# Twelve more first products in blocks, masks on GpSimd, and a refitted issue order in an attention and mixture kernel

## Chip, cores and metric

One core of a Trainium2 chip runs one program. The metric is device microseconds from launch to end, the median of several runs. Lower is better.

## The reference

Four batches of 768 tokens go through an attention of 8 heads (64 wide), and the result through four dense experts that are mixed by per-token shares.

```python
scores = (q @ k.T) / sqrt(D)
keep = (key < 4) | ((0 <= query - key) & (query - key < 128))      # 4 sinks and a window of 128
a = softmax(where(keep, scores, -1e9))
x = (a @ v)                                  # 3072 tokens x 512 (heads side by side)
p = domain_probs / (domain_probs.sum(-1) + 1e-9)
for e in range(4):
    h = maximum(x @ w1[e], 0)                # 512 -> 1024
    out += p[:, e] * (h @ w2[e])             # 1024 -> 512
```

## The kernel before, in words

Everything is in bf16 with f32 accumulation. A batch has 3 groups of 256 tokens, so there are 12 pairs (batch b, group g), and with 4 experts e 48 units (b, g, e). The first product of a unit is x @ w1[e], the second h @ w2[e].

**Attention.** Scores are made per group and pair of heads (`scores`, line 634 to 640), with keys on the partitions. ScalarE takes the exponential into the tile aT (L665). The window is then cut out by a mask: in batch 0 partly by a bias in PSUM or a multiplication of each head (L674), in batches 1 to 3 by one VectorE multiplication of both heads with a 0/1 mask (L659). Then come the value products (L706, with the sinks at L699), a reciprocal on VectorE (L733) and the scaling on ScalarE (L745). DMA transposes on the SP queue turn the rows of q and k (L220) and the attention's result (L723); six row buffers (qkn) are filled by loads from the POOL queue (L208), and values by L273. The POOL queue also holds a small copy, L1405, that waits for the last transpose of a batch's rows.

**First products.** Plain: 4 pieces of 8 matmuls with 256 columns (L1020), each evacuated with the rectifier and, from batch 1, the gate (L1044 on VectorE; in batch 0 L1033 on ScalarE or L1035 on VectorE). In blocks: a Strassen-Winograd form with 7 instead of 8 products of half size (`emit_fast`, L1098), 56 matmuls of 128 columns. It needs three combined forms of w1[e] (`weight_form1`) and four of the tokens, called T (L1072); two copies on ScalarE (L1126, L1139), an addition into PSUM (L1133), one out of it (L1148) and four gated evacuations on VectorE (L1117). START says from which batch an expert's first products are made in blocks: 18 units of experts 0 and 1, and 6 of experts 2 and 3, so 24.

**Second products.** Batch 0: plain, 512 columns (L1323), scaled and summed on VectorE (L1333, L1335). Batches 1 to 3: in blocks over the four experts together (L1252), from sums and differences of H made on VectorE (L1177, L1198), and with combined forms of w2 (`weight_form`); results are copied out at L1295, L1283 and L1288.

**Order.** The kernel is written out in a fixed order by a planner that runs while the program is built: it keeps a clock for each engine (t["pe"], t["dve"], t["pool"] ...) with a price for each operation. In its main loop it collects the steps that could be next on TensorE (attention, first, second, product), with the time when each would be ready and a rank, and emits the lowest rank of those that are ready. Evacuations, masks and forms are put into a list by `later` with a due time, and `flush` emits them when their engine is free. Each engine runs its instructions in the emitted order. Loads are taken from a list, head first.

Of the kernel before, what the change touches and what calls it, by code (L numbers as in the profile page):

```python
# [16 lines left out]
def kernel(  # L17
# [12 lines left out]
    nc = tc.nc  # L30
# [30 lines left out]
    START = {0: 1, 1: 1, 2: 3, 3: 3}  # L61
# [3 lines left out]
    BEHIND = 800  # L65
    CHORES = 3
    OWN = 2
    BIASED = 1
    FAST = tuple(START)
    UNITS = ("P1", "P5", "P6", "P2", "P7", "P3", "P4")  # L70
# [53 lines left out]
    def flush(until, once=False):  # L124

        ran = False
        while True:
            best = None
            for engine in ("act", "dve"):
                mine = [x for x in pend if x[2] in (engine, "any")]  # L130
                if not mine:
                    continue
                at = max(t[engine], min(x[0] for x in mine))
                if at <= until and (best is None or at < best[0]):
                    best = at, engine, min((x for x in mine if x[0] <= at), key=lambda x: x[1])
# [165 lines left out]
    def weight_form(e):  # L301

        w = w2_sb[e].rearrange("p (k f) (c d) -> p k c f d", k=2, c=2)
        if e not in forms:
            x = wpool.tile([P, 3, NFB // 2, Dout // 2], BF16, name=f"wf_{e}", tag=f"wf_{e}")
            forms[e] = {"P1": w[:, 0, 0], "P2": w[:, 1, 0], "P3": w[:, 1, 1], "P4": x[:, 2],
                        "P5": w[:, 0, 1], "P6": x[:, 0], "P7": x[:, 1]}
            formed[e] = 0
# [7 lines left out]
        else:  # L316
            nc.vector.tensor_sub(x["P5"], x["P5"], x["P1"])
        formed[e] += 1
        forms_at[e] = dve(1024, rate=1.92)

    forms1, formed1, forms1_at, left1 = {}, {}, {}, [NG * START.get(e, 0) for e in range(E)]

    def weight_form1(e):
# [3 lines left out]
        if e not in forms1:  # L327
            if e < OWN:
                x = wpool.tile([P, 3, NDB // 2, F // 2], BF16, name=f"vf_{e}", tag=f"vf_{e}")
                x = [x[:, i] for i in range(3)]  # L330
            else:
                x = [sb.tile([P, 2, H, D], BF16, name="qkn", tag="qkn", bufs=NQB) for _ in range(3)]
                x = [i.rearrange("p d h c -> p d (h c)") for i in x]
# [17 lines left out]
    def form1_due(e):  # L351
        n = formed1.get(e, 0)
        if e >= OWN and turned_at.get((B - 1, NQB - 1), 1e12) > t["pe"]:
            return False
        return landed.get(("w1", e), 1e12) + 4000 < t["pe"] and (n < 3 or n == 3 and not left1[e])

    def form_due(e):
        n = formed.get(e, 0)
        return landed.get(("w2", e), 1e12) + 9000 < t["pe"] and (n < 3 or n == 3 and e in used)
# [3 lines left out]
    def next_form():  # L363
# [12 lines left out]
        later("dve", t["pe"], 9000, run)  # L376
# [244 lines left out]
    def scores(b, hp, g, more=False):  # L621
# [34 lines left out]
        else:  # L656
            def mask_both(at):
# [3 lines left out]
                later("dve", at, 1500, run)  # L661
# [219 lines left out]
    class Mixture:  # L881


        def __init__(self):
# [3 lines left out]
            for b, g in PAIRS:  # L888
                fast = [e for e in range(E) if self.is_fast(b, e)]
# [17 lines left out]
        def is_fast(self, b, e):  # L907
            return b >= START.get(e, B)
# [14 lines left out]
        def early_ready(self, g):  # L923
            if not self.early[g] or not self.room():
                return 1e12
            xs = [xT_at.get((0, hp, g), 1e12) for hp in range(NHP)]
            e = self.early[g][0]
            return max([t["pe"], free_at(), landed.get(("w1", e, 0), landed.get(("w1", e), 1e12)), *xs])

        def opened(self, b, g, e):  # L930
# [7 lines left out]
            fast = self.is_fast(b, e)  # L938
# [11 lines left out]
        def begin(self):  # L950

            if self.open or any(self.early.values()):
                return
            if self.units and self.room():
                self.open.append(self.opened(*self.units.pop(0)))

        def widen(self):

            u = self.open[0]
            if len(self.open) == 1 and u["unit"][0] and len(u["left"]) < len(UNITS) and self.units and self.room():  # L960
                b, g, e = self.units[0]
                if u["fast"] and (not self.is_fast(b, e) or not att.more()) and u["unit"] not in self.early:
                    self.open.append(self.opened(*self.units.pop(0)))

        def firsts(self):

            self.begin()
            if not self.open:
                g = min(self.early, key=lambda g: (self.early_ready(g), self.early[g][:1], g))
                yield self.early_ready(g), ("early", g)  # L970
                return
            self.widen()
            for u in self.open:
                b, g, e = u["unit"]
                xs = [xT_at.get((b, hp, g), 1e12) for hp in range(NHP)]
                if u["fast"]:
                    if "P1" in u["left"]:
                        at = max(free_at(3), forms1_at.get(e, 1e12) if formed1.get(e, 0) == 4 else 1e12, *xs)
                        if (b, g) not in self.T_at:
                            at = 1e12  # L980
                        yield at, (u, "P1")
                        continue
                    for m in u["left"]:
                        yield u["at"].get(m, 1e12), (u, m)
                else:
                    j = u["left"][0]
                    w = landed.get(("w1", e, 0), 1e12) if j < QF // 2 else landed.get(("w1", e), 1e12)
                    yield max(free_at(), w, *xs), (u, j)

        def emit_first(self, what, ready):  # L990

            if what[0] == "early":
# [4 lines left out]
                j = 0  # L997
# [3 lines left out]
            if j == 0 and (b, e) == (0, E - 1) and not gate_sb:  # L1001
# [48 lines left out]
            later("dve", end, 500, run)  # L1050

        def tokens(self):

            pairs = [x for x in PAIRS if any(self.is_fast(x[0], e) for e in FAST)]
# [4 lines left out]
            if n > 1 and any((*pairs[n - 2], e) not in self.finished for e in range(E)):  # L1059
# [427 lines left out]
```

## Time and profile before

| what | value |
|---|---|
| runs | 367.1, 368.88, 369.92 us; median 368.88 |
| profiled execution: span from first to last instruction | 365.3 us (no other time of that execution is listed) |
| granted TensorE clock | 1.000 |
| TensorE, VectorE, ScalarE, GpSimd busy | 358.0, 282.5, 154.1, 71.7 us |
| VectorE masks of batches 1 to 3 (128x1024) | 24, 0.683 us each |
| GpSimd affine select (128x520, bf16) | 2, 0.706 us each |

How to read it: PE is TensorE's matmul, PEld its weight loads, DVE VectorE, ACT ScalarE, POOL GpSimd. A line of a group names the source line, the engine, the operation, what it writes and reads, and its count; then busy us and mean ns of one; then the idle time of the engine before it, and what ended that. Matmuls are pipelined, so a mean of 273 ns for one is its latency; the pace at which they issue is read from the chain of work, where lengths of runs of equal matmuls stand.

### The profile page before, as it was taken

The numbers are of one execution on the slowest core, as the hardware profiler recorded it, in microseconds if no ns is written. First come the engines' busy times: TensorE is split into PE (matmuls) and PEld (weight loads), VectorE is DVE, ScalarE is ACT, GpSimd is POOL, SyncE is SP. The second block draws the span as 40 slices with busy tenths as digits, with TensorE's granted clock in tenths as the row PEclk, the third lists the DMA queues.
The fourth block names the chain that finished last, engine by engine and source line by source line (L and its number), as shares of the span: only waits on it lengthen the run. The fifth ranks groups of instructions, "written<-read, shape, count | busy, mean of one in ns | idle before, by whom it ended". The sixth has DMA issues, their size and how long they took to land.

```text
span 365.3 us, 9873 instructions
## 1 busy us (share of the span) xinstructions
PE 358.0 (98%) x4117; PEld 297.0 (81%) x4117; DVE 282.5 (77%) x630; ACT 154.1 (42%) x396; POOL 71.7 (20%) x92
## 2 busy tenths in 40 slices
PE   8799999999999999999999999999999999999996
PEld 4485766667666888899988899899999999999995
DVE  6744995657653999789789979869899898899860
ACT  5844732587554356445345446452103213222110
POOL 8945117400842057001200000000000000000000
PEclk9999999999999999999999999999999999999999
DMA  9999999999999999917890031213012112020011
GB/s 164 173 183 196 210 211 155 138 155 136 157 145 169 172 167 153 112 41 80 161 178 25 16 103 31 45 45 88 21 23 75 31 45 60 16 74 2 2 59 57
DMA packets 117288, 37.20 MB, mean 102 GB/s; under 512 B 100612, under 2 KB 112740, under 8 KB 117244
## 3 DMA queue, kind: packets, MB, share of 16 engines
q0 software_dynamic: 77520, 17.31, 55.4%
q1 hardware_dynamic: 38668, 18.75, 27.3%
q8 instruction: 32, 0.52, 0.6%
q10 hardware_dynamic: 1056, 0.52, 0.5%
q14 instruction: 12, 0.10, 0.1%
HBM read 40.45 MB, written 6.34 MB: 128 GB/s over the span
## 4 chain that ended last, share of the span: by engine, by line
PE 91%; DVE 3%; DMA 2%; ACT 1%; issue 1%; DVEq 0%; ACTq 0%
PE acc L1252 29%; PE hps L1020 22%; PE cps L1098 20%; PE acc L1323 11%; PE od L706 3%; PE sps L640 3%; DMA w<-in_moe_w_dram 2%; PE acc L513 1%; PE od L699 1%; ACT aT L665 1%; DVE H L1044 1%; PE tx L764 0%; DVE H L1117 0%; DVE osb L1333 0%; PE tr L534 0%
## 5 line engine op out<-in xcount | busy, mean ns | idle before, releaser
L1020 PE MATMUL hps<-xT,w 128*128 128x256 bf16 x768 | 95.0, 273 | 1.6 <-DMA w<-in_moe_w_dram 1.6
L1020 PEld LDWEIGHTS <-w 128*128 128x128 bf16 x768 | 72.7, 98 | 14.5 <-issue 2.0
L1252 PEld LDWEIGHTS <-H 128*128 128x128 bf16 x600 | 56.0, 98 | 6.3 <-issue 0.7
L665 ACT ACTIVATE aT<-sps 128x512 bf16<-128x512 f32 (+1 forms) x96 | 47.0, 577 | 26.0 <-PE sps L640 25.9
L1098 PEld LDWEIGHTS <-w 128*128 128x128 bf16 x768 | 48.3, 98 | 2.3 <-issue 0.7
L1252 PE MATMUL acc<-w,H 128*128 128x256 bf16 x360 | 47.8, 273 | 0.0
L1323 PE MATMUL acc<-w,H 128*128 128x512 bf16 x192 | 45.4, 379 | 0.0
L745 ACT ACTIVATE onat<-od,R 128x64 bf16<-128x64 f32 x144 | 33.2, 325 | 26.6 <-DVE R L733 24.3
L1117 DVE SCALAR_TENSOR_TENSOR H<-cps,gates 128x512 bf16<-128x512 f32 x57 | 38.9, 686 | 2.1 <-PE cps L1098 0.9
L1295 ACT COPY osb<-acc 128x256 f32<-128x256 f32 x36 | 13.5, 374 | 60.0 <-PE acc L1252 57.9
L1033 ACT ACTIVATE H<-hps 128x512 bf16<-128x512 f32 x39 | 23.4, 599 | 34.7 <-PE hps L1020 34.5
L1044 DVE SCALAR_TENSOR_TENSOR H<-hps,gates 128x512 bf16<-128x512 f32 x44 | 30.0, 688 | 10.0 <-PE hps L1020 9.7
L1323 PEld LDWEIGHTS <-H 128*128 128x128 bf16 x192 | 18.1, 98 | 17.6 <-issue 0.2
L273 POOL DMA_DIRECT2D vx<-in_v_dram x24 | 21.4, 900 | 54.6 <-PE od L706 46.5
L1252 PE MATMUL acc<-wf,H 128*128 128x256 bf16 x240 | 32.1, 273 | 0.0
L1252 PEld LDWEIGHTS <-S 128*128 128x128 bf16 x288 | 27.0, 98 | 3.0 <-issue 0.3
L1098 PE MATMUL cps<-T,w 128*128 128x128 bf16 x384 | 29.3, 219 | 0.0
L1098 PE MATMUL cps<-xT,w 128*128 128x128 bf16 x384 | 29.1, 219 | 0.0
L1126 ACT COPY cps<-cps 128x512 f32<-128x512 f32 x24 | 13.8, 574 | 35.2 <-PE cps L1098 32.8
L1098 PEld LDWEIGHTS <-vf 128*128 128x128 bf16 x432 | 26.8, 98 | 0.9 <-issue 0.3
L1335 DVE SCALAR_TENSOR_TENSOR osb<-acc,scale_t,osb 128x512 f32<-128x512 f32 x18 | 13.5, 750 | 14.4 <-PE acc L1323 14.3
L659 DVE TENSOR_TENSOR aT<-aT,mask 128x1024 bf16<-128x1024 bf16 (+1 forms) x36 | 22.3, 639 | 0.7 <-ACT aT L665 0.6
(116 smaller groups left out, 514.2 us busy)
## 6 DMA issues: line engine op xcount, KB each, us to landing
w<-in_moe_w_dram POOLq DMA_DIRECT2D x7, 1024.0 KB, 16.0
out_dram<-osb SPq DMA_DIRECT2D x23, 256.0 KB
gates<-gate_rows SPq DMA_DIRECT2D x36, 128.0 KB
vx<-in_v_dram POOLq DMA_DIRECT2D x24, 128.0 KB, 10.9
qkn<-in_q_dram POOLq DMA_DIRECT2D x22, 128.0 KB, 9.5
qkn<-in_k_dram POOLq DMA_DIRECT2D x22, 128.0 KB, 9.7
w<-in_moe_w_dram POOLq DMA_DIRECT2D x2, 512.0 KB, 8.4
kraw<-in_k_dram ACTq DMA_DIRECT2D x2, 256.0 KB
```

The source lines that it names most:

```text
L273: nc.gpsimd.dma_start(out=vx[tb][:, :, 0:D], in_=v[b, :, tb * P:(tb + 1) * P, :].rearrange("h p d -> p h d"),)
L659: nc.vector.tensor_mul(a, a, m[:, None, :].to_broadcast([P, 2, w]))
L665: nc.scalar.activation(out=a[:, ph], in_=sps[ph][:, 0:w], func=AF.Exp, scale=scale)
L745: nc.scalar.mul(o[:, qi, hp, ph * D:(ph + 1) * D], od[:, qi, ph, 0:D], R[:, qi, ph])
L1020: nc.tensor.matmul(h[:, i].rearrange("p (q n) -> p q n", q=2), lhsT=w1_sb[e][:, db, fb * P:(fb + 1) * P], rhs=xT[b, g][:, :, db], start=(i ...
L1033: nc.scalar.activation(out=dst, in_=h, func=AF.Relu)
L1044: nc.vector.scalar_tensor_tensor(out=dst, in0=h, scalar=0.0, in1=gate, op0=ALU.max, op1=ALU.mult,)
L1098: nc.tensor.matmul(y[:, f], lhsT=A[:, d, f * P:(f + 1) * P], rhs=T[:, d], start=(m in ("P1", "P5") and f == 0 and d == 0), stop=(d == 1), ...
L1117: nc.vector.scalar_tensor_tensor(out=dst, in0=src, scalar=0.0, in1=gate, op0=ALU.max, op1=ALU.mult)
L1126: nc.scalar.copy(out=tiles["Y"], in_=y)
L1252: nc.tensor.matmul(x, lhsT=self.operand(b, g, e, m)[:, f], rhs=forms[e][m][:, f], start=(k == 0 and f == 0 and m in (("P1", "P5", "P2") if ...
L1323: nc.tensor.matmul(op, lhsT=H[:, fb // QF, fb % QF, s], rhs=w2_sb[e][:, fb, :], start=(fb == 0), stop=(fb == NFB - 1),)
```

## The change

START becomes a pair (batch, group) for each expert. Blocks now make 9 units of expert 0, 10 of expert 1, 12 of expert 2 and 5 of expert 3: 36 instead of 24, four of the twelve new ones in batch 0, where their evacuations have no gate and can go to ScalarE. The masks of groups 1 and 2 in batches 1 to 3 become two affine selects each on GpSimd, 48 in all (those of group 0 stay on VectorE). A bank of PSUM (V) is taken at P5 instead of at P1; the last evacuation of a unit waits also for the one before; a third T tile lies in an xT buffer. The forms of w2 of expert 3 and w1 of expert 3 lie in row buffers (three of the six each, after the transposes of batch 1 and of batch 3), and those of w1 of expert 2 in what was the place of w2's. Second products in blocks wait until batch 0 is done, and for the weight form that they use instead of all forms. Loads are taken from the list as they become ready, not only its head. The ranks and due times are refitted.

```diff
-    START = {0: 1, 1: 1, 2: 3, 3: 3}
+    START = {0: (1, 0), 1: (0, 2), 2: (0, 0), 3: (2, 1)}
+    MIX = 3
+    SHARE_OF = (1.01, 1.03, 1.05)
+    LEAD = (1.0, 1.0)
+    DUE = 1.5
+    LOW_PRODUCT = 2.015
+    HIGH_PRODUCT = -1
+    GATE = 3000
+    TOKEN = 2500
+    MARGIN = 4000
+    FULL = 7
+    WIDE = 2
+    OPEN = 2.2
-    BEHIND = 800
-    CHORES = 3
+    BEHIND = 2500
+    CHORES = 2
...
-            for engine in ("act", "dve"):
-                mine = [x for x in pend if x[2] in (engine, "any")]
+            for engine in ("act", "dve", "pool"):
+                mine = [x for x in pend if x[2] == engine or x[2] == "any" and engine != "pool"]
...
+    def spare_rows(e):
+
+        spared[e] = [sb.tile([P, 2, H, D], BF16, name="qkn", tag="qkn", bufs=NQB) for _ in range(3)]
+        spared_at[e] = qkn_free[2]
+        del qkn_free[0:3]
...
                 def run(engine):
                     nc.vector.tensor_mul(a, a, m[:, None, :].to_broadcast([P, 2, w]))
                     masked(dve(2 * w, rate=1.92))
-                later("dve", at, 1500, run)
+
+                def select(engine):
+                    x = a.rearrange("p h (n k q) -> p h n k q", n=2, k=2)
+                    for k, sgn in ((0, -1), (1, 1)):
+                        nc.gpsimd.affine_select(
+                            out=x[:, :, :, k], in_=x[:, :, :, k], compare_op=ALU.is_ge, fill=0.0,
+                            base=min(sgn, 0), pattern=[[0, 2], [0, 2], [sgn, P]], channel_multiplier=-sgn,
+                        )
+                        at = pool(0, fixed=705)
+                    masked(at + 60)
+                if g == 0:
+                    later("dve", at, 1500, run)
+                else:
+                    later("pool", at, 1500, select)
...
-        def is_fast(self, b, e):
-            return b >= START.get(e, B)
+        def is_fast(self, b, g, e):
+            return (b, g) >= START[e]
...
+            if n < WIDE and early:
+                at, g = self.next_early()
+                yield at, (OPEN if n else 2), ("early", g)
...
-                spare.sort(key=lambda i: (whole[i], ring[i]))
-                slots = u["slots"] = dict(zip("XV", spare[:2]), Y=spare[-1])
+                spare.sort(key=lambda i: (whole[i], ring[i]))
+                slots = u["slots"] = dict(X=spare[0], Y=spare[-1])
...
+            elif m == "P5":
+                spare = [i for i in range(6) if ring[i] <= ready + 40]
+                i = u["slots"]["V"] = min(spare, key=lambda i: (whole[i], ring[i]))
...
+                if b == 0:
+                    def relu(engine):
+                        if engine == "act":
+                            nc.scalar.activation(out=dst, in_=src, func=AF.Relu)
+                        else:
+                            nc.vector.tensor_scalar(out=dst, in0=src, scalar1=0.0, scalar2=None, op0=ALU.max)
...
-            return max(at, max(forms_at.values()) if sum(formed.values()) == 4 * E else 1e12)
+            if self.second or self.open and not self.open[0]["unit"][0] or any(self.early.values()):
+                return 1e12
+            return max(at, forms_at.get((e, m), 0.0 if m in ("P1", "P2", "P3") else 1e12))
...
-        if loads and t["pool"] < now + 1500 and load_ready(loads[0]) < now + 1500 and free_ring(loads[0]):
-            x = loads.pop(0)
+        x = next((x for x in loads if load_ready(x) < now + 1500), None)
+        if x and t["pool"] < now + 1500 and free_ring(x):
+            loads.remove(x)
             x[0](*x[1:])
...
+            if b in (1, B - 1) and x[1] == NQB - 1:
+                spare_rows("w2" if b == 1 else "w1")
...
-        opts.append((max(p, now), 1 if behind > BEHIND else 2.5, "product", None))
-        opts += [(max(f, now), 2, "first", x) for f, x in mix.firsts()]
-        opts.append((max(s2, now), 1 if mix.since >= 1 else 2.5, "second", None))
+        opts.append((max(p, now), HIGH_PRODUCT if behind > BEHIND or mix.live >= FULL else LOW_PRODUCT, "product", None))
+        opts += [(max(f, now), p, "first", x) for f, p, x in mix.firsts()]
+        opts.append((max(s2, now), 1 if mix.since >= 1 else LOW_SECOND, "second", None))
```

## The prediction

> **What bounds the kernel now.** First the busy table and the slices of the page: who is full, and where.
>
> ```profile
> PE 358.0 (98%) x4117; PEld 297.0 (81%) x4117; DVE 282.5 (77%) x630; ACT 154.1 (42%) x396; POOL 71.7 (20%) x92
> ...
> PE   8799999999999999999999999999999999999996
> ...
> DVE  6744995657653999789789979869899898899860
> ...
> POOL 8945117400842057001200000000000000000000
> PEclk9999999999999999999999999999999999999999
> ```
>
> PE is full in all slices but the first two and the last, at full clock. DVE is at 40 to 70% until slice 13 (119 us), and at 80 to 90% and more from there: it is the second limit. POOL is nearly idle after slice 20. A busy PE can still be slow, so next the chain that ended last, in order of time (start, length, what), which gives the pace of each kind of product:
>
> ```profile
> 56.02 2.62 PE hps L1020 x24
> 58.64 1.73 PE acc L1323 x8
> ...
> 282.23 1.79 PE cps L1098 x32
> ...
> 342.92 3.49 PE acc L1252 x32
> ```
>
> A plain first product (256 columns) issues every 2.62/24 = 0.109 us, one in blocks (128 columns) every 1.79/32 = 0.056, a second product every 3.49/32 = 0.109, a 512-column one every 1.73/8 = 0.216. 768 x 0.109 + 1344 x 0.056 + 1008 x 0.109 + 192 x 0.216 = 310 us of a span of 365.3; attention, transposes, the start and the end have the rest. From the starts of PE's rows in the trace, time above each shape's median pace is 4.4 us in the first 20 us (weights and rows still landing, where the order is not changed) and only about 7 us in all the rest. So the time is PE's work; waits are small change. The stages of DVE (length, then busy time and count of PE, PEld, DVE, ACT, POOL):
>
> ```profile
> 80.00:100.00 20.00, 20.00 (x205) 13.61 (x206) 13.12 (x29) 13.35 (x37) 8.94 (x11) 1.00 1.24 151
> ...
> 160.00:180.00 20.00, 20.00 (x255) 18.05 (x255) 18.38 (x43) 10.24 (x31) 1.76 (x2) 1.00 0.64 95
> ...
> 280.00:300.00 20.00, 20.00 (x268) 18.90 (x266) 18.21 (x37) 4.29 (x9) 0.00 (x0) 1.00 0.10 32
> ```
>
> The first batch leaves DVE a third free, batches 1 to 3 under a tenth.
>
> **The change part by part.** The profiled execution spans 365.3 us; the runs' median, 368.88, is 3.6 above it. I carry differences of the span over to the median unchanged.
>
> *PE work.* Twelve units change from 32 products of 256 columns to 56 of 128. Off: 384 x 0.109 = 41.9 us. On: 672 x 0.056 = 37.6, and two 512-column products that clear a bank, 2 x 0.216 = 0.4 (there were none). Net -3.9 us, all of it on the path, since PE is full. Other PE work has the same counts.
>
> *DVE and ACT.* Durations from these groups:
>
> ```profile
> L1117 DVE SCALAR_TENSOR_TENSOR H<-cps,gates 128x512 bf16<-128x512 f32 x57 | 38.9, 686 | 2.1 <-PE cps L1098 0.9
> ...
> L1044 DVE SCALAR_TENSOR_TENSOR H<-hps,gates 128x512 bf16<-128x512 f32 x44 | 30.0, 688 | 10.0 <-PE hps L1020 9.7
> ...
> L659 DVE TENSOR_TENSOR aT<-aT,mask 128x1024 bf16<-128x1024 bf16 x24 | 15.9, 683 | 0.1
> ...
> L446 POOL TENSOR_SCALAR_AFFINE_SELECT sel<-sel 128x520 bf16<-128x520 bf16 x2 | 1.4, 706 | 0.6 <-DVE sel L444 0.6
> ```
>
> DVE loses 37 evacuations of plain products (5 of them in batch 0) and 24 masks: 37 x 0.688 + 24 x 0.683 = 41.8. It gains 32 gated evacuations and 8 of batch 0, 12 additions into PSUM and 12 out of it (0.69 each), and 12 token forms (0.285): 64 x 0.687 + 3.4 = 47.4. Net +5.6, so 288 busy of about 361. The first four units fall where DVE is a third free. Places on PE are the paces above added up along the new PE order, with the first matmul of the attention put at 7 us and no waits. Laying the new DVE order beside it, with its durations scaled by what overlaps (their sum is 318, the busy time 282.5), DVE's load is about 0.83 while selects run (PE's 95th to 239th us), 1.02 from 239 to 270, and 0.94 from 239 to 324. The same count gives 0.96 for the old kernel's stretch of 163 to 208, in which PE lost about 1.3 us. So nothing here turns DVE into the bound for long, but its cover is thin; if it goes, the late thing is the addition into PSUM, for which the third and seventh block products wait in PE's order. ACT: 24 copies of 0.58 and 8 evacuations more, 11 evacuations fewer: +12 us on 154, covered, as ACT idles over half.
>
> *Selects on POOL.* 48 x 0.706 = 33.9 us on an engine with 71.7. Each pair waits for two exponentials of ACT; behind it in POOL's queue stand the next selects and, in batches 1 and 2, value and row loads (0.88 each). Tightest place: in batch 1, two value loads (1.8 us) stand between the first and second selects of the last group, and wait for the second group's value products. Those end at PE's 99.9; loads and selects take to 103.4; the next value product is placed at 103.7. Bounds: 0 if it fits, 1 to 2 us if the loads wait for an older landing; I take 0, as elsewhere 5 us and more lie between scores and values. In batch 3 no loads stand between.
>
> *Port.* What a select costs DVE is the unknown. At the start of the trace, two selects run from 2.37 to 3.85:
>
> ```profile
> 2.37 1.48 POOL L446 TENSOR_SCALAR_AFFINE_SELECT sel<-sel 128x520 bf16<-128x520 bf16 x2 [0.57 <-DVE sel L444]
> ```
> ```profile
> 3.39 0.55 DVE L467 TENSOR_SCALAR lent<-lent 128x256 bf16<-128x256 bf16 x1
> ...
> 13.21 0.28 DVE L482 TENSOR_SCALAR mask<-lent 128x512 bf16<-128x512 bf16 x1
> ```
>
> The 256-wide operation under a select took 0.55 us, twice the 0.28 of a 512-wide one with none: some 0.27 lost. Other operations may lose from 0 to a whole select: 0 to 33.9 us of DVE in all; at 0.27 each, 13. From 95 to 239 DVE has 24 us free (0.17 x 144), so 13 brings it to 0.92, under the 0.96 that cost 1.3 us in 45. I price it at +1 us, ends 0 and +10 (33.9 less the 24 free).
>
> The Trainium skill (SBUF — State Buffer, Who interferes with whom) speaks against the change: a VectorE instruction with two SBUF inputs and a GpSimd one that reads SBUF exclude each other for the whole instruction. No row here shows it for such a VectorE instruction. About half of DVE's busy time from 170 to 240 is of that kind, so an estimate by the page is 0.35 to 0.4 us a select, 17 to 19 us, more than the 16.4 that the masks took; the sum would be near 367.
>
> *Rows and DMA order.* Three of the six row buffers become weight forms after batch 1's transposes, so rows of batches 2 and 3 load in two lots of three; SP's 18 row transposes split accordingly (as 6, 1, 2, 1, 2 and 3, 1, 2 among gates and stores). A lot takes its 6 issues of 0.9 us, about 10 us to land and a transpose wait on SP; the second lot of batch 2 is issued at about 107 and needed at PE's 135, that of batch 3 about 165 against 201. 15 us of cover or more; if SP's queue of gates (longest wait on it now 11.7 us, on a gated evacuation) holds them, a few us. I take 0. SP gets no more DMAs. Weight form operations keep their number and width.
>
> *Refitted order.* It can take at most the 7 us of waits outside the first 20, or add as much. No row sizes it. I take -1, which is no more than the port's +1.
>
> Sum: -3.9 + 1 - 1 = -3.9; 368.9 - 3.9 = 365.0.
>
> **Rivals.**
> 1. DVE binds in the last batches. For: its load of 1.02 in 239 to 270 and 0.94 to the end of the first products. Against: 280 to 300 ran at 18.21 of 20 with no idle PE. At the old rate of 1.3 us lost in 45, 85 us lose 2.5: 367.5.
> 2. The port lock decides (the other side). Place: batches 1 to 3, under selects. Price: 48 selects of up to 0.706. Up to 0.5 us each (24 us) it hides in DVE's free time; at the full 0.706, 10 us come out on PE: 375. For: the 0.55 row. Against: it needs nearly every select to meet a conflicting operation from its start.
> 3. The refit also removes waits: half of the 7 us: 361.5 to 362.
> 4. The saving isn't there (the added block products slower than 0.056, as they are woven finer): at 0.0617 the gain is gone, 369. The old trace shows 0.056 in lots of 16 to 32 alike, so little for it.
>
> **How the numbers follow.** Forecast (365.0, give or take 1.7) 0.42; rival 1 0.18; rival 2 0.13; rival 3 0.22; rival 4 0.05. The range takes in rivals 1, 3 and 4 and the mild half of 2: 360.5 to 372. One per cent, about what a measurement can tell from no change, is 365.2 to 372.6. Below: rival 3 and a little over half of the forecast, 0.47. Above: rival 2 and a little, 0.14. Within: 0.39.
>
> **What would show it.** PE rows: 384 plain and 2016 block products at 0.109 and 0.056, chain shares of hps halved. DVE near 288 busy; if the port costs, two-input operations (0.419 for S forms) grow, and selects exceed 0.706. Rival 1 shows as PE idle after 240 released by DVE; rival 3 as less idle between 20 and 250. A wait of PE for POOL at the value products, or for row transposes, would prove the queue steps wrong.

## The result, and the profile after

| | before | after |
|---|---|---|
| median of 20 runs each, on one chip | 368.59 us (367.0 to 369.92) | 371.57 us (367.81 to 372.64) |
| ratio to before | 1 | 1.0081, 95% interval 1.0063 to 1.0098 |
| profiled execution: span | 365.3 us | 367.3 us |
| profiled execution: its own time | 367.1 us | 369.15 us |

The change made the kernel 0.8% slower, within the 1% that the prediction took as its bound. The forecast was 365.0, a gain of 3.9 us; it was 6.6 us too low and had the wrong sign, though the time lies inside the range. The two profiled executions differ by 2.0 us, so the traces show two thirds of the 3.0 between the medians.

First the busy table and the slices of the changed kernel.

```profile
PE 355.6 (97%) x4395; PEld 298.4 (81%) x4407; DVE 289.1 (79%) x645; ACT 164.1 (45%) x417; POOL 101.5 (28%) x140
...
PE   8799999999999999999999998999999999999986
...
DVE  6854998966787689689489969858999998987830
...
POOL 8945117303946408412830022220000000000000
PEclk9999999999999999999999999999999999999999
```

PE is busy for 2.4 us less than before, yet the span is 2.0 longer: PE waits more. DVE grew to 289.1 where 288 was predicted, ACT by 10.0 where 12 was. Next the chain that ended last of the changed kernel, in order of time, for the pace of each kind of product.

```profile
49.15 2.62 PE hps L1063 x24
...
118.64 3.49 PE hps L1063 x32
...
257.64 1.79 PE cps L1150 x32
...
300.12 3.06 PE acc L1324 x28
```

A plain piece still issues every 2.62/24 = 0.109 us, a block product every 1.79/32 = 0.056, a second product every 3.06/28 = 0.109. The trace has 384 plain first products and 2016 in blocks, as the change says. So the 3.9 us of removed work were delivered. Adding up, from the starts of PE's rows, the time above each shape's pace gives, by one count for both traces, 9.1 us before and 16.3 after: 7.2 us of new waits. Of them 0.3 lie in the first 40 us, 0.8, 1.8, 0.2 and 0.5 in the four stretches of 40 us up to 200, 2.2 from 200 to 240, 0.4 from 240 to 280, none from 280 to 320, and 1.1 from there to the end. (Minus 3.9 and plus 7.2 is 3.3 where the spans differ by 2.0; that is how well the count holds. It depends on how the paces are taken: the prediction's count of the trace before was 4.4 and 7, not 9.1.)

What those waits are is in the list of PE's waits. Before:

```profile
PE hps L1020 <- DMA w<-in_moe_w_dram: 1.6, 1, 1.6
PE acc L513 <- DVE lent L427: 1.4, 1, 1.4
PE od L706 <- ACT onat L745: 0.3, 1, 0.3
PE sps L640 <- ACT aT L665: 0.2, 1, 0.2
```

And after (us in total, times, longest):

```profile
PE hps L1063 <- DMA w<-in_moe_w_dram: 1.7, 1, 1.7
PE acc L549 <- DVE lent L463: 1.4, 1, 1.4
PE acc L1324 <- ACT osb L1367: 1.0, 1, 1.0
PE cps L1150 <- DVE H L1218: 0.7, 1, 0.7
PE cps L1150 <- ACT onat L794: 0.6, 2, 0.3
PE sps L676 <- ACT onat L794: 0.4, 1, 0.4
PE cps L1150 <- DVE cps L1203: 0.4, 1, 0.4
PE od L755 <- ACT onat L794: 0.2, 1, 0.2
...
PE od L748 <- ACT onat L794: 0.2, 1, 0.2
```

The first two, in the first 20 us, are those of before. New are three kinds. ScalarE's scaling of the attention (onat, L794) stands in four lines, 1.4 us; with the shorter gaps that the list leaves out, the count above gives it 3.3 us after 20 us, and 0.7 before. VectorE's additions of the block products (L1218, L1203) give 1.7 by the count. One wait of 1.0 to 1.2 us at the end is for the copy of the last pair's result (osb, L1367). No wait is for POOL and none for a row transpose. The stages, in the columns of the prediction:

```profile
80.00:100.00 20.00, 19.84 (x200) 13.16 (x203) 13.25 (x25) 10.41 (x26) 11.27 (x16) 1.00 1.42 159
...
220.00:240.00 20.00, 18.55 (x262) 16.11 (x261) 18.02 (x38) 10.77 (x29) 4.91 (x8) 1.00 0.17 42
280.00:300.00 20.00, 20.00 (x289) 19.14 (x287) 18.96 (x39) 5.93 (x13) 0.00 (x0) 1.00 0.13 41
```

PE idles where selects run (POOL 4.91 in 220 to 240) and where attention is still made, and not from 280 to 320, where DVE has the most to do.

**The two new waits in rows.** A set of four scalings, and the block product that waits for it, in the timeline of the changed kernel (start, length, engine, operation; in brackets the wait before it): the reciprocal on VectorE, the scalings on ScalarE, and PE's work beside and behind them.

```profile
250.16 0.17 DVE L782 RECIPROCAL R<-od 128x4 f32<-128x4 f32 x1
...
250.37 0.93 ACT L794 ACTIVATE onat<-od,R 128x64 bf16<-128x64 f32 x4 [0.79 <-DVE R L782]
...
250.44 0.60 PE L1324 MATMUL acc<-w,H 128*128 128x256 bf16 x4
...
251.35 0.61 PE L1150 MATMUL cps<-xT,w 128*128 128x128 bf16 x8 [0.30 <-ACT onat L794]
```

The scaling reads od in one of six PSUM banks that attention and block products share in a ring. It ends at 251.30, and the block product that gets a bank starts at 251.35. ScalarE was idle before it: the engine is not short of time, the set just takes 0.93 us. The planner counts 4 x 0.128 = 0.51 us of ScalarE for it (75 ns and 64 columns at 1.2 a ns each), and has the bank free 0.64 us after the start, as it adds 130 ns behind the last.

VectorE under selects, and then without, in the timeline of the changed kernel, the selects first:

```profile
225.54 1.28 POOL L701 TENSOR_SCALAR_AFFINE_SELECT aT<-aT 128x512 bf16<-128x512 bf16 x2 [0.71 <-ACT aT L714]
```
```profile
225.62 0.70 DVE L1119 TENSOR_TENSOR T<-xT 128x256 bf16<-128x256 bf16 x1
226.36 0.60 DVE L1119 TENSOR_TENSOR T<-xT,T 128x256 bf16<-128x256 bf16 x1
226.88 0.28 DVE L1119 TENSOR_TENSOR T<-xT 128x256 bf16<-128x256 bf16 x1
```

An operation of the same shape takes 0.70 us under a select and 0.28 just after it. So the port costs something where they meet; how much in all was for the experiments.

### The profile page after: what moved, and what is told of

Same layout as the page of the kernel before. It is cut to its first block, busy times and chain, and to the rows that moved or that the text cites. A ratio compares the mean times of both kernels' runs of the same rounds, so it can differ in the third digit from the quotient of the medians.

```text
span 367.3 us, 10580 instructions
## 1 busy us (share of the span) xinstructions
PE 355.6 (97%) x4395; PEld 298.4 (81%) x4407; DVE 289.1 (79%) x645; ACT 164.1 (45%) x417; POOL 101.5 (28%) x140
## 4 chain that ended last, share of the span: by engine, by line
PE 80%; DVE 9%; ACT 6%; DMA 3%; issue 1%; DVEq 0%; ACTq 0%
PE acc L1324 27%; PE cps L1150 26%; PE acc L1395 10%; PE hps L1063 9%; ACT onat L794 3%; DVE H L1183 3%; PE sps L676 2%; DMA w<-in_moe_w_dram 2%; PE od L755 2%; ACT aT L714 2%; PE acc L549 1%; DVE H L1218 1%; DVE S L1268 1%; DMA out_dram<-osb 1%; DVE T L1119 1%
## 5 line engine op out<-in xcount | busy, mean ns | idle before, releaser
L1150 PEld LDWEIGHTS <-w 128*128 128x128 bf16 x1152 | 71.6, 98 | 5.6 <-issue 3.3
L1183 DVE SCALAR_TENSOR_TENSOR H<-cps,gates 128x512 bf16<-128x512 f32 x78 | 52.4, 682 | 0.7
L1063 PE MATMUL hps<-xT,w 128*128 128x256 bf16 x384 | 47.5, 273 | 1.7 <-DMA w<-in_moe_w_dram 1.7
L1150 PEld LDWEIGHTS <-vf 128*128 128x128 bf16 x744 | 45.7, 98 | 2.3 <-issue 1.0
L701 POOL TENSOR_SCALAR_AFFINE_SELECT aT<-aT 128x512 bf16<-128x512 bf16 x48 | 30.2, 664 | 59.3 <-ACT aT L714 25.2
L794 ACT ACTIVATE onat<-od,R 128x64 bf16<-128x64 f32 x144 | 33.3, 324 | 28.7 <-DVE R L782 25.6
L1150 PE MATMUL cps<-T,w 128*128 128x128 bf16 x576 | 43.8, 219 | 0.9 <-DVE H L1218 0.7
L1150 PE MATMUL cps<-xT,w 128*128 128x128 bf16 x576 | 43.6, 219 | 0.8 <-DVE cps L1203 0.4
L1063 PEld LDWEIGHTS <-w 128*128 128x128 bf16 x384 | 35.9, 98 | 8.3 <-DMA w<-in_moe_w_dram 1.9
L1367 ACT COPY osb<-acc 128x256 f32<-128x256 f32 x36 | 13.5, 375 | 53.8 <-PE acc L1324 50.0
L1150 PE MATMUL cps<-T,vf 128*128 128x128 bf16 x496 | 36.9, 219 | 0.3 <-ACT onat L794 0.3
L1203 DVE TENSOR_TENSOR cps<-H,cps 128x512 f32<-128x512 f32 x30 | 20.8, 692 | 7.2 <-PE cps L1150 5.9
L1218 DVE TENSOR_TENSOR H<-H,cps 128x512 f32<-128x512 f32 x30 | 20.5, 684 | 6.5 <-PE cps L1150 6.3
```

Source lines behind the costliest of these rows:

```text
L701: nc.gpsimd.affine_select(out=x[:, :, :, k], in_=x[:, :, :, k], compare_op=ALU.is_ge, fill=0.0, base=min(sgn, 0), pattern=[[0, 2], [0, 2], ...
L794: nc.scalar.mul(o[:, qi, hp, ph * D:(ph + 1) * D], od[:, qi, ph, 0:D], R[:, qi, ph])
L1063: nc.tensor.matmul(h[:, i].rearrange("p (q n) -> p q n", q=2), lhsT=w1_sb[e][:, db, fb * P:(fb + 1) * P], rhs=xT[b, g][:, :, db], start=(i ...
L1150: nc.tensor.matmul(y[:, f], lhsT=A[:, d, f * P:(f + 1) * P], rhs=T[:, d], start=(m in ("P1", "P5") and f == 0 and d == 0), stop=(d == 1), ...
L1183: nc.vector.scalar_tensor_tensor(out=dst, in0=src, scalar=0.0, in1=gate, op0=ALU.max, op1=ALU.mult)
L1203: nc.vector.tensor_add(tiles["V"], c5, tiles["X"])
```

## The experiments

The theories. **A**: the scalings on ScalarE, priced at nothing, free PSUM banks too late. **B** (the forecast's second rival): the selects take VectorE's port, and its additions come late. **C** (its first rival): VectorE has too much to do in the last batches. **D**: the new order is simply worse, by many small waits. "Order held" means that the planner's clock was advanced as in the changed kernel, so that every other instruction keeps its place. Ratios are to the kernel before, with 95% intervals; the changed kernel stands at 1.0081. Differences from it in us are ratio differences times 368.6; by the intervals, they are uncertain by 1.1 to 1.3 us either way (by 2 for the kernel with selects made twice).

### Taking one cost away, order held

**Selects left out, and doubled.**

```diff
-                        nc.gpsimd.affine_select(...)
```
```diff
+                        for _ in range(2):
                             nc.gpsimd.affine_select(...)
```

> The changed kernel with the 48 affine selects left out (so the window isn't cut out in groups 1 and 2 of batches 1 to 3); the order on PE, DVE, ACT and SP is the same row by row. In the changed kernel VectorE's two-input operations are longer than before (H<-H,S 460 against 417 ns, T 332 against 285), some 5.5 us in all. Theory 'port': the selects hold up VectorE, and PE then waits for it; without them S and T forms go back to 419 and 285 ns and the time falls by 2 to 4 us, to 367.5 to 369.5, the waits between 200 and 240 us gone. Rival 'order': the waits are in the new order itself (slots that ScalarE frees late, chains with too little between them); the time stays within 0.7 us of the changed kernel's.

> Every select is run twice (the second changes nothing); all other engines' order is the same. Theory 'port': VectorE loses another 5 us and PE another 2 to 5 us, time 373.5 to 377. Rival 'order': selects have slack enough and VectorE too; up to 1 us more. If it is much more than what leaving them out gains, masks came late for the value products, which would show as PE waiting for POOL.

Without selects: 369.42 us, 1.002 (0.999 to 1.005), 2.2 us less. Twice: 377.05, 1.0249 (1.0197 to 1.0301), 6.2 us more. The groups without selects, as in the table of costliest groups:

```profile
L1264 DVE TENSOR_TENSOR H<-H 128x512 bf16<-128x512 bf16 x30 | 12.4, 418 | 0.0
L1243 DVE TENSOR_TENSOR H<-H,S 128x512 bf16<-128x512 bf16 x30 | 11.4, 417 | 0.0
L1115 DVE TENSOR_TENSOR T<-xT,T 128x256 bf16<-128x256 bf16 x24 | 6.9, 286 | 0.4
```

The same three in the changed kernel, and its selects:

```profile
L1268 DVE TENSOR_TENSOR H<-H 128x512 bf16<-128x512 bf16 x30 | 13.3, 448 | 0.0
L1247 DVE TENSOR_TENSOR H<-H,S 128x512 bf16<-128x512 bf16 x30 | 12.7, 460 | 0.0
L1119 DVE TENSOR_TENSOR T<-xT,T 128x256 bf16<-128x256 bf16 x24 | 8.0, 332 | 0.4
...
L701 POOL TENSOR_SCALAR_AFFINE_SELECT aT<-aT 128x512 bf16<-128x512 bf16 x48 | 30.2, 664 | 59.3 <-ACT aT L714 25.2 <-DVE osb L1355 24.9 <-DVE H L1183 9.2
```

Operations of VectorE with two bf16 inputs from SBUF are longer with selects, and hardly any others: the gated evacuations from PSUM kept 682 ns, and those from SBUF 683 (684 without selects). DVE's busy time is 289.1 with and 284.9 without, and the lengthened groups sum to 4.8 us. That is 4.8/48 = 0.10 us a select. The second lot of 48 lengthened VectorE's busy time by 8.6 us more, 0.18 each, so the cost of a select is no constant. The select itself took 0.664 where 0.706 was priced. PE's waits for L1218 fall from 0.9 to 0.2 us without the selects; those for scalings stay at 3.3. B is real, and a third of what was lost against the forecast. Twice the selects shows how little room was left (PE's waits, the three longest new kinds):

```profile
PE acc L1325 <- DVE osb L1361: 3.2, 2, 2.3
PE od L756 <- POOL aT L702: 1.9, 3, 1.1
PE sps L676 <- DMA qkT<-qkn: 1.7, 1, 1.7
```

**Four scalings made one copy**, in the changed kernel and, as a control, in the kernel before; and both costs taken from the changed kernel.

```diff
-                        nc.scalar.mul(o[:, qi, hp, ph * D:(ph + 1) * D], od[:, qi, ph, 0:D], R[:, qi, ph])
...
+                nc.scalar.copy(out=o[:, :, hp].rearrange("p q (h d) -> p q h d", h=2), in_=od[:, :, :, 0:D])
```

> The four multiplications on ScalarE that scale a value product (0.93 us together) become one copy of about 0.4 us, so the softmax's normalisation is left out in batches 1 to 3; the order is otherwise the same. Rival 'ScalarE': in the changed kernel's trace several PE waits (0.2 to 0.7 us each, at 77, 112, 134, 230 and 250 us) end with these multiplications, because they free a PSUM slot or stand in front of a block product's copy; without them 1.5 to 3 us come back, 368.5 to 370. Theory 'port': under 0.7 us.

> Control for the run that scaled with one copy: the kernel before, with the same edit (normalisation left out in batches 1 to 3, ScalarE relieved of some 19 us), order held. In the changed kernel the edit gave 4.2 us (371.57 to 367.36). If ScalarE became tight only with the twelve new units (48 more uses of it: 24 copies, and their rush), the kernel before gains under 1 us (0.997 or more). If scaling blocks were as costly before, it gains 3 us or more (0.992 or less), and ScalarE explains none of the loss.

> The changed kernel without the 48 selects and with scaling by one copy, both as before (window mask and normalisation left out in places), order held. Alone they gave 2.2 and 4.2 us. If the two delays are separate, 6.4 us: 365.2, a ratio to the kernel before of 0.991, which is the forecast of the prediction. If they are the same slack used twice (VectorE and ScalarE hand on to each other), 4 to 5 us: 366.5 to 367.5.

Changed kernel: 367.36, 0.9967 (0.994 to 0.9995), 4.2 us less. Kernel before: 367.82, 0.9979 (0.9957 to 1.0001), 0.8 less. Both costs away: 366.49, 0.993 (0.9905 to 0.9955), 5.6 less than the changed kernel. The groups of the scalings in the kernel before, in the changed kernel and with one copy:

```profile
L745 ACT ACTIVATE onat<-od,R 128x64 bf16<-128x64 f32 x144 | 33.2, 325 | 26.6 <-DVE R L733 24.3
```
```profile
L794 ACT ACTIVATE onat<-od,R 128x64 bf16<-128x64 f32 x144 | 33.3, 324 | 28.7 <-DVE R L782 25.6
```
```profile
L792 ACT CAST onat<-od 128x256 bf16<-128x256 f32 x36 | 13.4, 375 | 31.4 <-DVE R L782 28.6 <-PE acc L1394 2.7
```

The one copy took 0.375 us instead of a set's 0.93, ACT's busy time fell to 145.2, and all waits of PE for the scalings were gone. The copy doesn't read R, but in the trace it still waits for the reciprocal, and starts some 0.03 us behind it as a set does; so what the edit takes away is time of ScalarE, and no wait for VectorE. The same slow step, equally long in both, costs the kernel before 0.8 us and the changed one 4.2: 3.4 of the loss (give or take 1.4) are A, on an engine that is idle more than half of the time.

**The last pair's result in a buffer of its own**, so that its copy does not wait for the store of the pair before.

```diff
-                out_sb[b, g] = mo.tile([P, 2, Dout], FP32, name="osb", tag="osb", bufs=1)
+                out_sb[b, g] = wpool.tile([P, 2, Dout], FP32, name="osbl", tag=f"w1_{E - 1}") if final else mo.tile(...)
```

> The output buffer of the last pair lies in expert 3's w1 weights (no longer needed) instead of the one buffer of all pairs, so that the last pair's first copy needn't wait for the store of the pair before; order unchanged. In the changed kernel PE waits 1.0 us there at 354 us, in the one before it doesn't. If that wait is a steady part of the loss, the time falls by 1 us, to 370.5; if it was chance of one execution, by under 0.4.

370.8, 1.0063 (1.0034 to 1.0092): 0.7 us less, which is not clear of noise. The wait itself is plain in the timeline of the changed kernel, where ScalarE's second copy at the end waits for the store:

```profile
350.87 0.37 ACT L1367 COPY osb<-acc 128x256 f32<-128x256 f32 x1 [4.87 <-PE acc L1324]
354.91 0.37 ACT L1367 COPY osb<-acc 128x256 f32<-128x256 f32 x1 [3.67 <-DMA out_dram<-osb]
```

Before, it waited 2.16 us there, and cost PE nothing that its list of waits shows:

```profile
352.50 0.37 ACT L1295 COPY osb<-acc 128x256 f32<-128x256 f32 x1 [2.16 <-DMA out_dram<-osb]
```

**All three away** (no selects, one scaling, last buffer), order held:

> The changed kernel, order held, without the selects, with scaling by one copy (window mask and normalisation left out in batches 1 to 3) and with the last pair's own output buffer. Without the first two it was 0.993. If the three delays are what stood between forecast and result, 0.989 to 0.991 (the forecast's 365.0 is 0.990 of the kernel before). If the buffer's wait is not a steady loss, 0.993 again, and some 2 us stay spread over small waits of the new order.

364.84, 0.9897 (0.9866 to 0.9927), span 363.3: 6.8 us less than the changed kernel, and the time that was forecast. PE's waits in its trace:

```profile
PE sps L676 <- DMA qkT<-qkn: 1.8, 1, 1.8
PE acc L549 <- DVE lent L463: 1.4, 1, 1.4
PE hps L1058 <- DMA w<-in_moe_w_dram: 1.4, 1, 1.4
```

Its stage of 220 to 240, where the changed kernel's PE had 18.55:

```profile
220.00:240.00 20.00, 19.99 (x275) 17.63 (x275) 17.08 (x39) 10.58 (x22) 0.00 (x0) 1.00 0.17 39
```

The fair comparison is with the kernel before when its scalings are one copy too (0.9979): 0.9897/0.9979 = 0.9918, 3.0 us of gain (give or take 1.4), near the 3.9 less of PE's work. It still has no masks, which the control has. That the time meets the forecast's 365.0 is partly chance: this version does less work than the forecast was for. With the three costs away a new wait appears in the same order, 1.8 us for a row transpose.

### Planning anew

**The old START in the changed planner** (24 units), and **all masks on VectorE**.

```diff
-    START = {0: (1, 0), 1: (0, 2), 2: (0, 0), 3: (2, 1)}
+    START = {0: (1, 0), 1: (1, 0), 2: (3, 0), 3: (3, 0)}
```
```diff
-                if g == 0:
+                if True:
```

> The changed kernel with the old choice of units in blocks (24, none in batch 0), selects on GpSimd and all refitted constants kept; the order is planned anew. PE's work is 3.9 us more. If the new units bring what PE's sum says, 375 (1.019). If their extra uses of VectorE (5.6 with the masks' gain, 22 without) and ScalarE (12 us) bring waits that eat it, the time is about that of the changed kernel or less, 369 to 372; at 368.5 or less the refit and selects would be neutral and the twelve units the loss.

> The changed kernel with all masks of batches 1 to 3 multiplied on VectorE again (24 x 0.683 us back on it, 48 selects and 5 us of lengthened forms gone); 36 units in blocks and constants kept, order planned anew. VectorE then has 289 - 5 + 16 = 300 busy. Theory 'port': selects cost 5 and save 16, so they are still worth it: 373 to 375. Rival: VectorE's free time covers 11 us more and the selects' lateness was the larger ill: 369 to 371.

Old START: 376.62, 1.0206 (1.0168 to 1.0244). Under the same constants the kernel with the twelve units is 4.6 us faster, of which 3.9 are PE's work by the sum above. But the constants were fitted with these units, and with the old ones the order has longer waits (3.2 us for weights instead of 1.7, and 1.9 for a mask on VectorE), so this measures neither the units nor the refit alone. Masks on VectorE: 369.76, 1.0033 (1.0008 to 1.0058), 1.8 us less than with selects, though VectorE's busy time is then 299.7. Two things weaken this run. The new order also has fewer waits for scalings (one of 0.4 us in the list, where the changed kernel has five of 1.4 together), so the 1.8 us are not the masks' alone. And this order, like the one with the true price alone below, does not give the reference's result, for a reason that is not known: a wait that a right order needs may be missing from its time.

**The selects alone, in the kernel before** (its constants and START):

> The kernel before with one part of the change: masks of groups 1 and 2 in batches 1 to 3 as 48 affine selects on GpSimd, planned anew with its own constants; 24 units in blocks. VectorE is relieved of 16 us and loses some 5 to the selects. Theory 'port' as the runs so far have it (a select costs PE more than it gives where VectorE is near its limit; masks on VectorE were 1.8 us faster in the changed kernel): 1 to 3 us slower than before, 1.003 to 1.008. If the selects are harmless by themselves and only the dense new order made them bite: 0.997 to 1.002.

377.29, 1.0221 (1.0184 to 1.0258), far over what any theory gave. Its stages with the loss:

```profile
120.00:140.00 20.00, 18.96 (x250) 15.86 (x249) 17.89 (x40) 8.47 (x29) 9.63 (x13) 1.00 1.45 185
140.00:160.00 20.00, 18.17 (x181) 14.49 (x179) 17.89 (x35) 9.41 (x27) 10.22 (x15) 0.91 1.36 100
```

In them the POOL queue holds the copy that waits for transposes, 12 row loads and 4 value loads ahead of batch 2's first selects (at 145.34). There is also a granted clock of 0.91 in the second. The clock explains little of it: the two runs with a mean granted clock of 0.995 took 375.69 and 376.53 us, and the kernel before at 0.995 a median of 368.55. For the queue, no wait of PE in these 40 us is put down to POOL. So the cause of the 8 us stays open.

**The true price of a scaling in the planner** (170 columns' worth instead of 64 gives 0.22 us), in the changed kernel, in the kernel before, and in the changed kernel with masks on VectorE:

```diff
-                        at = act(D)
+                        at = act(170)
```

> The changed kernel with the planner's price for one scaling multiplication on ScalarE put right: 217 ns from start to start instead of 128 (a block of four takes 0.93 us in the trace and 0.51 in the plan), order planned anew. In the changed kernel's trace PE loses 3.3 us to waits that end with these multiplications, 0.7 in the kernel before. Theory 'price': the plan believed that PSUM slots and ScalarE come free 0.4 us sooner than they do, and with half of the plain pieces gone nothing covers it; with the right price 2 to 3.5 us come back: 368 to 369.6. Rival: ScalarE is short whatever the plan knows: within 1 us of 371.6.

> Control: the kernel before with the same price put right, planned anew. It loses 0.7 us to these waits, so 0 to 0.7 us come back (0.998 to 1.000); a change of over 1 us either way would show that any new plan of this kernel moves the time by that much, whatever the price.

> The changed kernel with the right price for scaling and with all masks of batches 1 to 3 on VectorE: 36 units in blocks, no selects. With the price alone 2 to 3.5 us and the masks back 1.8 us, if they add: 366 to 368, a ratio of 0.993 to 0.998, faster than the kernel before. If VectorE, now at 300 us busy, is the next limit: 369 to 370.

The changed kernel: 370.52, 1.0047 (1.0017 to 1.0076). The kernel before: 367.67, 0.9979 (0.9947 to 1.0011). With masks on VectorE: 368.66, 1.0004 (0.9972 to 1.0036), 2.8 us less than the changed kernel, with nothing left out and VectorE busy for 298.6 us: VectorE's load is not what limits, against C. In the first, PE's waits for scalings fell by the count from 3.3 to 0.7 us, but the time only by 1.2: waits for L1218 (1.6), for osb (0.9) and for S (0.7) took their place. This was a miss for A as I had put it: knowing the price moves the waits, it does not remove the latency.

**From there (36 units, true price, masks on VectorE, 1.0004), one thing more each:** each scaling planned as its own step with the last buffer; no masks of groups 1 and 2, order held; one scaling, order held; the last buffer, order held. And the split scalings in the kernel before.

```diff
-                        nc.scalar.mul(o[:, qi, hp, ph * D:(ph + 1) * D], od[:, qi, ph, 0:D], R[:, qi, ph])
-                        at = act(D)
...
+                qi, ph = parts.pop(0)
+                nc.scalar.mul(o[:, qi, hp, ph * D:(ph + 1) * D], od[:, qi, ph, 0:D], R[:, qi, ph])
+                at = act(170)
+                if parts:
+                    later("act", t["act"], 600, multiply)
```
```diff
+                    if g == 0:
                         nc.vector.tensor_mul(a, a, m[:, None, :].to_broadcast([P, 2, w]))
```

> 36 units in blocks, all masks on VectorE, the last pair's own output buffer, and each of the four scaling multiplications planned by itself at its right price, so that a block product's copy can go between them (delay at most 0.2 us, not 0.9). Theory 'ScalarE latency': 1.5 to 3 us less than with blocks of four (368.7): 365.5 to 367, 0.992 to 0.996. Theory 'VectorE load': only the store's 1 us: 367.5 to 368.5.

> Control: the kernel before with the four scaling multiplications planned one by one at the right price. It waits only 0.7 us on them; with the price alone it was 0.9979. Expected 0.997 to 1.000 on every theory.

> The kernel with the right price and masks on VectorE (368.66), with the 24 mask multiplications of groups 1 and 2 in batches 1 to 3 left out (window not cut out there), order held: VectorE is relieved of 16.4 us, nothing else changes. Theory 'VectorE load': 2 to 4 us less, 364.7 to 366.7. Theory 'ScalarE latency': within 1 us.

> The same kernel (right price, masks on VectorE, 368.66), with the four scaling multiplications as one copy (normalisation left out in batches 1 to 3), order held. PE's waits that end with the multiplications are 1.0 us in it. Theory 'ScalarE latency': 2 to 3 us less, 365.7 to 366.7; theory 'VectorE load': at most the control's 0.8 us.

> The kernel with the right price and masks on VectorE (1.0004) with the last pair's own output buffer, order held. PE waits 1.1 us for ScalarE's copy into that buffer in its trace. If that is steady: 367.5, 0.997; if not, 1.000.

| version | us | ratio to before | theory said |
|---|---|---|---|
| split scalings and last buffer | 368.61 | 1.0002 (0.9971 to 1.0034) | A: 365.5 to 367, a miss |
| split scalings in the kernel before | 370.35 | 1.0063 (1.003 to 1.0096) | 0.997 to 1.000, a miss |
| no masks of groups 1 and 2 | 368.46 | 0.9999 (0.9966 to 1.0033) | C: 2 to 4 us less, a miss; A: no change |
| one scaling | 367.35 | 0.9972 (0.9942 to 1.0001) | A: 2 to 3 us less, a miss |
| last buffer | 368.48 | 1.0 (0.9968 to 1.0032) | 0.997 if the wait is a steady loss, else 1.000: it is not |

Taking 24 masks off VectorE gains nothing, the second mark against C. But A does not hold in this order either: one scaling gives 1.2 us, hardly more than the 0.8 of the kernel before. And the last buffer gives nothing, though PE's wait for it is gone from the list. This kernel has 3.9 us less of PE's work than the kernel before and takes as long, and none of the three removals finds where that goes; it stays open. Each of the two replanned orders with split scalings has a new wait for row transposes, in the changed kernel and in the one before:

```profile
PE sps L676 <- DMA qkT<-qkn: 2.1, 1, 2.1
```
```profile
PE sinks L601 <- DMA qkT<-qkn: 3.1, 1, 3.1
```

So a new order can bring waits of 2 to 3 us that the planner does not price. That is what is left of D, and it limits what a replanned experiment can tell. With the whole computation done, no version beat the kernel before by more than its interval.

## Why the prediction was wrong, point by point

- *PE work, -3.9.* Right: counts and paces are as said, and with three costs away 3.0 of it come out against the control.
- *DVE and ACT, 0: the step that failed.* It said of ACT: "+12 us on 154, covered, as ACT idles over half." The +12 was nearly right (+10.0); the cover was not. An engine's idle share says that it can take more work, not that one piece of work is done in time. A set of scalings takes 0.93 us with ScalarE idle before it, and ends a bank's use that the next block product or score needs. Measured: 4.2 us in the changed kernel less 0.8 in the one before, 3.4 instead of 0. Why the same step costs more there is not shown. A unit in blocks takes its banks from the same ring, and there are 36 instead of 24, so a late bank can meet a waiting product more often; but with the same 36 units in another order (true price, masks on VectorE) it cost 1.2 us, so the number of units alone does not decide it. I named for each edit the work that hides it, but for this one named no buffer that it frees.
- *DVE, +5.6, 288 busy.* 289.1 was measured, but the match is luck: the +5.6 did not hold the port's cost, and without selects the busy time is 284.9, +2.4. Its load does not bind: no idle PE from 280 to 320, and no gain from removing masks.
- *Port, +1.* Right in kind, too low in time: 2.2 us (give or take 1.3). Per select it was overestimated (0.27 priced, 0.10 measured), but I set it against VectorE's free time in a whole stage, and each select delays the additions that PE waits for at once. The Trainium skill (SBUF — State Buffer, Who interferes with whom) has the direction right: 0.70 beside 0.28 in the rows, and the groups with two bf16 inputs from SBUF are longer. The estimate by that page of 0.35 to 0.4 us a select is over three times the 0.10 measured; how the prediction's sum near 367 follows from it is not worked out. Selects that meet evacuations from PSUM, whose groups kept their length (682 ns with selects and without), may be why, but that was not tested. That selects cost more than masks on VectorE, as that estimate has it, fits two runs in different orders: 2.2 us gained without selects, nothing gained without the masks.
- *Selects in POOL's queue, 0.* Right here: PE waits for POOL nowhere. With twice the selects it does, for 1.9 us.
- *Rows and DMA order, 0.* Right here, no wait on row transposes; in two other orders it was 2 to 3 us, and in this order 1.8 us once the three costs were away.
- *The end.* Not in the working at all: the last pair's copy behind the store of the pair before, a wait of 1.0 to 1.2 on PE. Its worth is not clear of noise: 0.7 us alone, 1.2 on top of the other two, none in the other order.
- *Refit, -1.* No such gain, and the prediction had no row for it. PE's waits rose by 7 us; the refit cannot be separated, since old units under new constants and the selects under old constants are both 2% slower.
- *Rivals.* The second was the right kind, at a third of the loss (its 375 adds its 10 us to the port's +1; by its own terms it is 374). The first, third and fourth did not occur. Missing was the one that took the most: an engine with idle time that answers late.

Sum with the measured sizes: -3.9 + 3.4 + 2.2 + 0.7 = +2.4, and +3.0 was measured. The three costs were 7.1 us taken singly (4.2 for the scalings) and 6.8 together.

## What to carry to other kernels

When a change thickens the main engine's work, price each step of an idle engine by its latency, from its input to the buffer that it frees, and ask who needs that buffer next; the idle share answers another question. A kernel whose bound engine waits for only some 9 of 365 us has little room in which a small lateness can hide. To test such a term, take the work away with the order held, and do the same in the kernel before: replanned versions move by 2 us and more for reasons of their own. And try it in a second order, as the cost found in one (4.2 us here) can be small in another (1.2).

## What the runs showed of the hardware

- An affine select of 128x512 bf16 took 0.664 us on average (0.702 when each was made twice).
- Four ScalarE operations of 128x64 from PSUM took 0.93 us, one of 128x256 took 0.375.
- The second store of the pair before the last, for which the copy of the last pair waits, landed 3.5 us after its issue in the changed kernel, and 2.0 us before. Before, it was issued 2.2 us behind the first store, and 1.3 us in the changed kernel. Whether that is the cause was not tried.
- Runs of the kernel before with a mean granted clock of 0.995 took 1.5 to 1.8 us longer than those at 1.0, by the medians of five lots of its runs; the changed kernel's 1.1 us (371.71 and 370.6). In the profile of the run with the true price the granted clock is 0.63 from 18 to 20 us, 0.52 from 20 to 22, and 1.00 beside that.
